# Attention ahead of two expert layers on one Trainium2 core: the turn back of a pair's outputs stands right ahead of the next pair's first products

## The chip, the core and the metric

The kernel runs on one core of a Trainium2 chip. It has five engines with a queue of instructions each: TensorE (PE in the profile; its weight loads are listed as PEld), VectorE (DVE), ScalarE (ACT), GpSimd (POOL) and SyncE (SP), which here issues most transfers. Engines wait for each other by semaphores alone. The metric is the time of one execution on the device in microseconds (us), the median of several runs; less is better.

## The reference, cut to what matters

Attention with normalized queries and keys, four batches of twelve heads, 448 tokens, 64 numbers a head; its output goes through a layer of eight experts of which each token takes one, and then through a dense layer of two matrices. The change lies in the attention alone.

```python
q_n, k_n = (rmsnorm(q, g_q), rmsnorm(k, g_k))
scores = scale * np.matmul(q_n, k_n.transpose(0, 1, 3, 2))
scores = scores - np.max(scores, axis=-1, keepdims=True)
attn = np.exp(scores)
attn = attn / (np.sum(attn, axis=-1, keepdims=True) + 1e-09)
return np.matmul(attn, v).astype(np.float32)
...
x = _moe_ref(x=x, **moe_kwargs)
return _moe2_ref(x=x, **moe2_kwargs)
```

## The kernel before

Attention goes by 24 pairs of heads. The 2 x 448 tokens of a pair are seven blocks of 128 (the fourth holds the last 64 tokens of both heads). The loop `for n in range(N)` runs over 168 steps, seven for each pair. In step n it writes out, in this order: the transpositions of one block of probabilities of the pair before (`turn_p`, line 306, into the tile "pt"), the scores of one block (`scores`, line 286, into "s"), the exponential of the block of the step before (`expo`, line 297, ScalarE), the copy of the transposed block out of PSUM (`take_p`, lines 326 and 328, ScalarE or VectorE), the maximum of the new block (`row_max`, line 291, VectorE), and then what the table `sched` holds for this step. There is no scheduler behind it: each engine works through its instructions in the order in which they are written, and a function that is put at a step adds its instructions to the queues of all engines that it uses, at that place.

The table is filled by `put(z + off, f, p)`, with z = 7p the first step of pair p's scores. What matters here, in steps 0 to 6 of the pair whose scores are being computed:

- `turn_k` (line 234) transposes the seven blocks of k on TensorE, four of them in step 2 and three in step 4, two pairs ahead or less, and ScalarE takes the high part (line 236); `k_low` (line 241) on VectorE takes the low part from the same PSUM tile "tk", in step 3 for the first four and in step 5 for the other three. After `k_low` nothing reads that tile.
- `turn_q` (line 217) transposes blocks of q in steps 5 and 3 into a PSUM tile "tq", which ScalarE copies out (lines 219, 222, 223).
- `mix` multiplies v with the transposed probabilities into the tile "av": blocks 0, 4, 1 and 5 in step 4 (line 338, weights of 128x64), the rest in step 6 (lines 338 and 342). `mixed` (line 347) copies the sum to the tile "osb" in step 6.
- `back`, the turn back, brings a pair's outputs, which have tokens along the columns, back to tokens along the rows, and multiplies them with the router's weights in the same passes: six full-size passes (three matmuls, line 363) and four quarter-size ones (two matmuls, line 365, weights of 64x64) into the PSUM tile "xo". `finish` calls `finish_pair`, in which VectorE scales the result in three operations (lines 1605, 1607, 1608). After a batch's last pair SyncE stores the batch (lines 1611, 1614), and the router's work on it is added in small pieces to later steps.

A float32 matmul stands in the profile as two passes with a weight load each, so the three matmuls of line 363 are six there. The tiles tk, tq and xo, and small ones of the router, belong to one PSUM group with the name "tq" and two buffers: a new tile takes a buffer that a former one has had, and its first matmul waits until the former one's last reader is done. The first pairs are placed by the table `place`, since the stage starts there; the last steps, with the turn back of pairs 22 and 23, are written out by hand behind the loop.

Of the kernel before, what the change touches and what calls it, by code (L numbers as in the profile page):

```python
# [32 lines left out]
def attention(tc, ctx, q, k, v, const, ps, late, finish_pair, tick, early):  # L33
# [352 lines left out]
    def put(n, f, p, *a):  # L386
        m = place.get(p, {}).get(f.__name__, n)
        sched.setdefault(m if type(m) is int else m[a[0]], []).append((f, (p,) + a))
# [13 lines left out]
    for p in range(NP):  # L402
        z = 7 * p
        put(z + 11, mix, p, (0, 1))
        put(z + 13, mix, p, (2, 3))
        for off, f in ((-16, scale_k), (-15, scale_q), (-13, q_high), (-12, q_low), (13, invert), (13, mixed), (15, back), (15, finish)):
            put(z + off, f, p)
        put(z - 7, load, p, "v")
        if 1 < p < 4:
            put(z - 14, copy_k, p)  # L410
        for off, f, i in ((-9, turn_q, 0), (-5, turn_k, 0), (-4, turn_q, 1), (-4, k_low, 0), (-3, turn_k, 1), (-2, k_low, 1)):
            put(z + off, f, p, i)
# [1122 lines left out]
def tile_kernel(ctx: ExitStack, tc: tile.TileContext, q, k, v, g_q, g_k, moe_modality_id, moe_w_gate, moe_modality_bias,  # L1535
                moe_w1, moe_w2, moe2_w_in, moe2_w_out, out):
    nc = tc.nc
    with tc.manual_schedule():
# [8 lines left out]
        with ExitStack() as c0:  # L1547
# [87 lines left out]

            moe.ident = moe.m.ident = ident
            attention(tc, c0, q, k, v, dict(ident=ident, identr=identr, comb=comb, gg=gg), ps, late, finish_pair, tick, lambda i: moe.early(i))
        moe.run(steps)

# [30 lines left out]
```

## Time and profile before

| | us |
|---|---|
| median of 3 runs | 1143.63 |
| lowest and highest | 1143.36, 1143.73 |
| the profiled execution | 1144.76 |
| its span, first to last instruction | 1142.8 |
| TensorE busy in the span | 1124.5 (98%) |
| VectorE, ScalarE, GpSimd busy | 822.6, 677.7, 368.4 |

Attention takes about the first 335 us of the span; the steady run of its steps is the stretch from 40 to 334 us. The sum of the busy times of an engine says little by itself; in the timeline a row is one or several equal instructions in a line, with the start of the first, the time until the end of the last, and in brackets how long the engine had been idle before and what ended that. Matmuls overlap, so the cost of one is the distance from its start to the next one's start.

### The profile page before, as it was taken

What the parts mean: (1) busy time and instruction counts of PE and PEld (TensorE: products, weight loads), DVE (VectorE), ACT (ScalarE), POOL (GpSimd) and SP (SyncE); (2) the same over time, 40 slices, a digit from 0 to 9 for tenths busy, and PEclk for the clock granted to TensorE, in tenths of its full rate; (3) what the DMA queues carried; (4) which work ended last, traced back from release to release, by engine and by line L of the source; (5) the groups of instructions that cost most, each with busy time, mean ns of one, the idle gap of its engine ahead of it and who ended that gap; (6) DMA issues with size and microseconds to landing.
All of it is one profiled execution on the core that took longest, in us unless ns stands there. A gap on an engine that the chain in (4) does not pass through costs nothing. (4 is left out here: it accounts for less than half of the span.)

```text
span 1142.8 us, 20023 instructions
## 1 busy us (share of the span) xinstructions
PE 1124.5 (98%) x7101; PEld 952.3 (83%) x7101; DVE 822.6 (72%) x1537; ACT 677.7 (59%) x1374; POOL 368.4 (32%) x559
## 2 busy tenths in 40 slices
PE   7999999999999999999999999999999999999997
PEld 6767777776768998999999988888888888888996
DVE  7887877867767667898989978884544455444674
ACT  6887777777654566666565555554543454433664
POOL 4575656644213204345644434430200010000100
PEclk9999999999999999999999999999999999999999
DMA  4343334213336789998999723330200011000100
GB/s 108 80 105 107 80 79 118 66 49 96 96 104 209 238 261 315 287 321 286 299 286 298 248 79 110 99 123 1 111 1 1 1 42 42 1 1 1 56 1 28
DMA packets 144708, 138.12 MB, mean 121 GB/s; under 512 B 39254, under 2 KB 125270, under 8 KB 144092
## 3 DMA queue, kind: packets, MB, share of 16 engines
q1 hardware_dynamic: 140444, 120.24, 34.7%
q0 software_dynamic: 4000, 16.53, 4.1%
q8 instruction: 57, 0.93, 0.4%
q14 instruction: 47, 0.39, 0.1%
q10 hardware_dynamic: 160, 0.03, 0.0%
HBM read 117.23 MB, written 18.10 MB: 118 GB/s over the span
## 5 line engine op out<-in xcount | busy, mean ns | idle before, releaser
L965 DVE TENSOR_TENSOR l<-ld,h 128x768 fp32r<-128x768 f32 x157 | 149.4, 968 | 18.7 <-ACT h L960 16.0
L1005 PE MATMUL a<-h,gh 128*128 128x512 f32 x476 | 159.4, 340 | 0.0
L1005 PE MATMUL a<-h,gl 128*128 128x512 f32 x476 | 157.7, 337 | 0.0
L1005 PE MATMUL a<-l,gh 128*128 128x512 f32 x476 | 157.7, 337 | 0.0
L937 POOL TENSOR_SCALAR cva<-cva 128x384 f32<-128x384 f32 x64 | 108.2, 1692 | 142.8 <-ACT cva L936 142.6
L960 ACT ACTIVATE h<-ld 128x768 fp32r<-128x768 f32 x159 | 130.6, 840 | 16.6 <-PE hs L984 6.5
L1479 POOL DMA_INDIRECT out_dram<-ld,oidx x11 | 12.8, 1159 | 334.4 <-DVE ld L1477 179.9
L297 ACT ACTIVATE P<-s,nb 128x448 f32<-128x448 f32 x144 | 91.7, 637 | 30.4 <-DVE nb L291 26.0
L291 DVE TENSOR_REDUCE nb<-s 128x1 f32<-128x448 f32 x168 | 102.9, 615 | 8.9 <-PE s L286 8.2
L1423 ACT ACTIVATE u<-hp,half 128x512 f32<-128x512 f32 (+1 forms) x64 | 40.4, 632 | 106.2 <-PE hp L973 106.2
L1430 DVE SCALAR_TENSOR_TENSOR w<-u 128x512 f32<-128x512 f32 (+1 forms) x64 | 40.2, 629 | 84.9 <-ACT u L1423 84.9
L1005 PEld LDWEIGHTS a<-h,gl 128*128 128x128 f32 x476 | 89.0, 189 | 10.7
L1005 PEld LDWEIGHTS a<-h,gh 128*128 128x128 f32 x476 | 89.0, 189 | 10.6
L1005 PEld LDWEIGHTS a<-l,gh 128*128 128x128 f32 x476 | 88.9, 189 | 9.6
L328 DVE COPY pT<-pt 128x448 f32<-128x448 f32 x96 | 59.8, 623 | 51.1 <-PE pt L306 51.1
L973 PE MATMUL hp<-yh,h 128*128 128x512 f32 (+1 forms) x384 | 88.5, 366 | 0.4 <-PEq L1372 0.4
L973 PE MATMUL hp<-yl,h 128*128 128x512 f32 (+1 forms) x384 | 87.2, 362 | 0.0
L973 PE MATMUL hp<-yh,l 128*128 128x512 f32 (+1 forms) x384 | 87.2, 362 | 0.0
L1438 DVE TENSOR_TENSOR gl<-u,gh 128x512 fp32r<-128x512 f32 (+1 forms) x64 | 40.0, 625 | 61.4 <-ACT gh L1437 61.4
L1181 ACT ACTIVATE rh<-hp 128x256 fp32r<-128x256 f32 x64 | 24.6, 384 | 100.3 <-PE hp L973 100.3
L306 PE MATMUL pt<-ident,P 128*128 128x128 f32 x504 | 83.4, 274 | 0.4 <-ACT P L297 0.2
L1437 ACT ACTIVATE gh<-u 128x512 fp32r<-128x512 f32 (+1 forms) x64 | 36.9, 577 | 77.5 <-PE a L1005 75.0
(345 smaller groups left out, 2821.0 us busy)
## 6 DMA issues: line engine op xcount, KB each, us to landing
ld<-in_moe_w_dram SPq DMA_DIRECT2D x160, 384.0 KB
raw<-in_moe_w_in_dram SPq DMA_DIRECT2D x32, 384.0 KB
ld<-in_moe_w_out_dram SPq DMA_DIRECT2D x26, 384.0 KB
rawk<-in_k_dram SPq DMA_DIRECT2D x24, 192.0 KB
rawq<-in_q_dram SPq DMA_DIRECT2D x24, 192.0 KB
rawv<-in_v_dram SPq DMA_DIRECT2D x24, 192.0 KB
xt_d<-x SPq DMA_DIRECT2D x4, 1152.0 KB
kn<-kn SPq DMA_DIRECT2D x20, 224.0 KB
```

The lines of the kernel that those rows point to most:

```text
L291: nc.vector.tensor_reduce(out=R["nb"][:, u:u + 1], in_=R["s", u], op=ALU.max, axis=AX.X, negate=True)
L297: nc.scalar.activation(out=o, in_=R.pop(("s", u)), func=ACTF.Exp, bias=R["nb"][:, u:u + 1], accum_out=R["sum"][:, w:w + 1])
L306: nc.tensor.transpose(out=out, in_=src, identity=ident)
L328: nc.vector.tensor_copy(out=R["PT", m], in_=t)
L937: nc.gpsimd.tensor_scalar(out=R["a"], in0=R["a"], scalar1=2.0 ** -15, scalar2=122879.9921875, op0=ALU.max, op1=ALU.min)
L960: nc.scalar.activation(out=h, in_=src, func=ACTF.Copy)
L965: (engine or self.nc.vector).tensor_tensor(out=l, in0=src, in1=h.bitcast(F32), op=ALU.subtract)
L973: nc.tensor.matmul(out=t[:, 0:n], lhsT=w[:, k], rhs=x[:, k, 0:n], start=i == 0 and k == 0, stop=i == 2 and k == 5)
L1005: nc.tensor.matmul(out=a[2][:, 256 * j:256 * j + 256] if c else a[j], lhsT=p[:, t * 128:t * 128 + 128], rhs=q[:, 512:768] if c else q[:, 0 ...
L1423: nc.scalar.activation(out=u, in_=t[:, s], func=ACTF.Relu, scale=0.5, bias=half)
L1430: nc.vector.scalar_tensor_tensor(out=w, in0=u, scalar=1.0, in1=u, op0=ALU.min, op1=ALU.mult)
L1438: nc.vector.tensor_tensor(out=gl[:, 0:n], in0=u, in1=gh[:, 0:n].bitcast(F32), op=ALU.subtract)
```

## The change

In the table, the offset of `back` and `finish` goes from 15 to 18. So the turn back of pair p leaves step 1 of pair p+2 and stands in step 4 of that pair. The `mix` of blocks 0, 4, 1 and 5 of pair p+1 is put at the same step (7(p+1) + 11 = 7p + 18) and comes behind it, since the table is filled pair by pair. For p up to 21 the step lies in the loop; pairs 22 and 23 are in the part written by hand, which is the same.

```diff
-        for off, f in ((-16, scale_k), (-15, scale_q), (-13, q_high), (-12, q_low), (13, invert), (13, mixed), (15, back), (15, finish)):
+        for off, f in ((-16, scale_k), (-15, scale_q), (-13, q_high), (-12, q_low), (13, invert), (13, mixed), (18, back), (18, finish)):
             put(z + off, f, p)
```

TensorE, step 1 of pair 11, where pair 9's turn back stood (s: scores, kh, kl and Q: the transposed k and q, xo: the turn back's tile, osb: the pair's outputs; a semaphore in brackets is one that the instruction waits for, by the engine that raises it). Before:

```order
L286 MATMUL s_2559<-kl_2401,Q_2280 128x448
L363 MATMUL xo_2569<-comb_89,osb_2521 128x144 [waits DVE_49]
L363 MATMUL xo_2569<-comb_89,osb_2521 128x144 x2
L365 MATMUL xo_2569<-comb_89,osb_2521 64x72 x2
L306 MATMUL pt_2580<-ident_70,pm1_274 128x128 [waits DVE_49]
L306 MATMUL pt_2580<-ident_70,P_2326 128x128 x3
```

The same place with the change:

```order
L286 MATMUL s_2559<-kh_2391,Q_2280 128x448
L286 MATMUL s_2559<-kl_2392,Q_2280 128x448
L306 MATMUL pt_2571<-ident_70,pm1_274 128x128 [waits DVE_49]
L306 MATMUL pt_2571<-ident_70,P_2326 128x128 x3
L286 MATMUL s_2576<-kh_2391,Q_2280 128x448
```

The two rows of the turn back are gone; the transpositions follow the scores.

TensorE, step 4 of the same pair, where the first products of pair 10 stand (av, from pT, the transposed probabilities, and rawv). Before:

```order
L286 MATMUL s_2626<-kh_2400,Q_2280 128x448 [waits Activation_49]
L286 MATMUL s_2626<-kl_2401,Q_2280 128x448
L338 MATMUL av_2633<-pT_2475,rawv_2145 64x448 [waits DMAHW2_49]
L338 MATMUL av_2633<-pT_2589,rawv_2145 64x448
L338 MATMUL av_2633<-pT_2506,rawv_2145 64x448
L338 MATMUL av_2633<-pT_2612,rawv_2145 64x448 [waits Activation_49]
```

With the change:

```order
L286 MATMUL s_2617<-kh_2391,Q_2280 128x448 [waits Activation_49]
L286 MATMUL s_2617<-kl_2392,Q_2280 128x448
L363 MATMUL xo_2624<-comb_89,osb_2521 128x144 [waits DVE_49,PE_49]
L363 MATMUL xo_2624<-comb_89,osb_2521 128x144 x2
L365 MATMUL xo_2624<-comb_89,osb_2521 64x72 x2
L338 MATMUL av_2633<-pT_2475,rawv_2145 64x448 [waits DMAHW2_49]
L338 MATMUL av_2633<-pT_2580,rawv_2145 64x448
L338 MATMUL av_2633<-pT_2506,rawv_2145 64x448
L338 MATMUL av_2633<-pT_2603,rawv_2145 64x448 [waits Activation_49]
```

The turn back stands between the scores and the products. Its first matmul waits for VectorE and for TensorE's own earlier writes; by the program's counts the VectorE instruction is the `k_low` of kl_2584 below.

VectorE, steps 1 to 4 of the same pair (nb: row_max, kl: k_low, x, lg and xt: the scaled outputs). Before:

```order
L291 TENSOR_REDUCE nb_2532<-s_2559 128x1 [waits PE_49]
L1605 TENSOR_TENSOR x_1954<-xo_2569,r_2519 128x3x128 [waits DVE_49,PE_49]
L1607 TENSOR_TENSOR lg_1956<-xo_2569,r_2519 128x7x8
L1608 TENSOR_SCALAR xt_1955<-xo_2569,r_2519 128x64
L328 COPY pT_2589<-pt_2580 128x448 [waits PE_49]
L291 TENSOR_REDUCE nb_2532<-s_2585 128x1 [waits PE_49]
L291 TENSOR_REDUCE nb_2532<-s_2606 128x1 [waits PE_49]
L241 SCALAR_TENSOR_TENSOR kl_2593<-tk_2594,gg_92,kh_2592 128x512 [waits Activation_49]
L328 COPY pT_2630<-pt_2621 128x448 [waits PE_49]
L291 TENSOR_REDUCE nb_2532<-s_2626 128x1 [waits PE_49]
```

With the change:

```order
L291 TENSOR_REDUCE nb_2532<-s_2559 128x1 [waits PE_49]
L328 COPY pT_2580<-pt_2571 128x448 [waits PE_49]
L291 TENSOR_REDUCE nb_2532<-s_2576 128x1 [waits PE_49]
L291 TENSOR_REDUCE nb_2532<-s_2597 128x1 [waits PE_49]
L241 SCALAR_TENSOR_TENSOR kl_2584<-tk_2585,gg_92,kh_2583 128x512 [waits Activation_49]
L328 COPY pT_2621<-pt_2612 128x448 [waits PE_49]
L291 TENSOR_REDUCE nb_2532<-s_2617 128x1 [waits PE_49]
L1605 TENSOR_TENSOR x_2037<-xo_2624,r_2519 128x3x128 [waits DVE_49,PE_49]
L1607 TENSOR_TENSOR lg_2039<-xo_2624,r_2519 128x7x8
L1608 TENSOR_SCALAR xt_2038<-xo_2624,r_2519 128x64
```

The three scaling operations move behind the row_max of step 4, past two copies, three row_max and the k_low.

On SyncE the stores of lines 1611 and 1614 stay where they were in its queue; ScalarE's and GpSimd's instructions keep their order.

## Rows read from the trace of the kernel before

**Rows 1.** Table by stretches: length; busy PE, PEld, DVE, ACT, POOL; clock; DMA share; GB/s.

```profile
12.00:18.00 6.00, 4.54 (x19) 3.73 (x20) 4.29 (x11) 4.17 (x12) 3.10 (x13) 0.72 0.45 86
40.00:334.00 294.00, 293.10 (x2008) 210.71 (x2006) 223.78 (x566) 220.51 (x588) 154.33 (x334) 1.00 0.31 85
```

**Rows 2.** TensorE's waits, 40 to 334 us: total us, times, longest.

```profile
PE pt L306 <- ACT pT L326: 0.2, 1, 0.2
```

**Rows 3.** Timeline, TensorE, pair 9's turn back: start, us, operation.

```profile
157.73 0.37 PE L286 MATMUL s<-kl,Q 128*128 128x448 f32 x1
157.94 0.90 PE L363 MATMUL xo<-comb,osb 128*128 128x144 f32 x6
158.76 0.34 PE L365 MATMUL xo<-comb,osb 64*64 64x72 f32 x4
159.04 0.33 PE L306 MATMUL pt<-ident,pm 128*128 128x128 f32 x1
159.20 0.49 PE L306 MATMUL pt<-ident,P 128*128 128x128 f32 x3
```

**Rows 4.** Timeline, TensorE, a step without a turn back.

```profile
182.16 0.37 PE L286 MATMUL s<-kl,Q 128*128 128x448 f32 x1
182.37 0.38 PE L306 MATMUL pt<-ident,pm 128*128 128x128 f32 x2
182.58 0.54 PE L306 MATMUL pt<-ident,P 128*128 128x128 f32 x3
```

**Rows 5.** Timeline, TensorE, steps 3 and 4 after pair 9's turn back.

```profile
161.43 0.37 PE L286 MATMUL s<-kl,qm 128*128 128x448 f32 x1
...
162.52 0.36 PE L286 MATMUL s<-kl,Q 128*128 128x448 f32 x1
162.81 1.72 PE L338 MATMUL av<-pT,rawv 128*64 128x448 f32 x8
```

**Rows 6.** Timeline, VectorE, the same steps, idle time in brackets.

```profile
159.16 0.56 DVE L1605 TENSOR_TENSOR x<-xo,r 128x384 f32<-128x384 f32 x1 [0.39 <-PE xo L365]
...
159.75 0.28 DVE L1608 TENSOR_SCALAR xt<-xo,r 128x64 f32<-128x64 f32 x1
...
161.84 0.62 DVE L291 TENSOR_REDUCE nb<-s 128x1 f32<-128x448 f32 x1 [0.75 <-PE s L286]
162.38 0.74 DVE L241 SCALAR_TENSOR_TENSOR kl<-tk,gg,kh 128x512 fp32r<-128x512 f32 x1
```

**Rows 7.** Timeline, first products and tile's reader, pairs 2, 6, 7, 8, 20.

```profile
71.21 1.84 PE L338 MATMUL av<-pT,rawv 128*64 128x448 f32 x8
...
72.40 0.24 ACT L223 ACTIVATE qm<-tq 128x64 fp32r<-128x64 f32 x1
...
122.98 0.97 PE L338 MATMUL av<-pT,rawv 128*64 128x448 f32 x4
...
122.77 0.74 DVE L241 SCALAR_TENSOR_TENSOR kl<-tk,gg,kh 128x512 fp32r<-128x512 f32 x1
...
136.12 1.35 PE L338 MATMUL av<-pT,rawv 128*64 128x448 f32 x6
...
136.38 0.74 DVE L241 SCALAR_TENSOR_TENSOR kl<-tk,gg,kh 128x512 fp32r<-128x512 f32 x1
...
149.27 0.97 PE L338 MATMUL av<-pT,rawv 128*64 128x448 f32 x4
...
149.20 0.73 DVE L241 SCALAR_TENSOR_TENSOR kl<-tk,gg,kh 128x512 fp32r<-128x512 f32 x1
...
305.64 0.60 PE L338 MATMUL av<-pT,rawv 128*64 128x448 f32 x2
...
305.35 0.49 ACT L219 ACTIVATE Q<-tq 128x384 fp32r<-128x384 f32 x1
```

**Rows 8.** Timeline, VectorE and TensorE's weight loads, a wait for k_low.

```profile
72.72 0.74 DVE L241 SCALAR_TENSOR_TENSOR kl<-tk,gg,kh 128x512 fp32r<-128x512 f32 x1
...
73.52 0.31 PEld L234 LDWEIGHTS tk<-ident,kn 128*128 128x128 f32 x3 [0.23 <-DVE kl L241]
```

## The prediction

> **What bounds the kernel now.** First the table by stretches: from 40 to 334 us, the attention stage in its steady run, TensorE is busy for 293.10 of 294.00 us at a granted clock of 1.00, which is its 2.4 GHz level; VectorE has 223.78 and ScalarE 220.51 [rows 1]. Then what TensorE waited for in that stretch: one entry of 0.2 us [rows 2]. So the stage is one queue of TensorE instructions without holes, in which the other engines' results are always there in time. Two things follow. What the change saves on TensorE itself is saved from the span, and any wait that it puts into that queue is added to the span in full, since no later hole takes it up. The timeline of TensorE around one turn back is the third view: the distances from start to start, not the busy times, are what an instruction costs there. The fourth is VectorE's timeline in the same steps.
>
> A pair of heads takes seven steps. I call them steps 0 to 6 of the pair whose scores are computed. Before, the turn back of pair p stands at the end of step 1 of pair p+2; now it stands in step 4 of pair p+2, right ahead of the first products of pair p+1. The move is made for pairs 0 to 21. Pairs 22 and 23 stand in the hand-written tail in both kernels.
>
> **The change part by part.**
>
> *What leaves step 1.* From the last scores matmul to the first turn-back matmul 0.21 us, six full-size ones 0.82, the four quarter-size ones 0.28 until the next transposition starts, and that first transposition takes 0.16 to the next one [rows 3]. Where scores are followed by transpositions directly, it is 0.21 and then 0.21 for two, so 0.105 for one [rows 4]. So 0.21 + 0.82 + 0.28 + 0.16 becomes 0.21 + 0.105: **1.155 us less**.
>
> *What enters step 4.* Scores to the first product takes 0.29 us now [rows 5]. It becomes 0.21 + 0.82 to the quarter-size matmuls and then their step to the products. No row shows quarter-size weights (64x64) followed by the products' half-size ones (128x64). The nearest row is quarter-size to full-size, 0.28 [rows 3]; a change of size between scores and products costs 0.29 where none costs 0.21 [rows 4, 5], and what follows the first instruction after one starts 0.055 later (0.16 for 0.105). I take 0.28: **1.02 us more**. Had this passage no price of its own, it would be about 0.135 less per pair, 3.0 us in all. By the Trainium skill (TensorEngine Tiling (Array Packing), Key Properties) a change of the tiling mode drains TensorE, and moving on within one mode does not; 64x64 and 128x64 are two modes there, so by that rule too the passage has its price.
>
> Balance of TensorE's own work: 1.02 - 1.155 = -0.135 us a pair, for 22 pairs **-3.0 us**. Were this all, the change would be a small gain.
>
> *The wait that it brings.* The turn back writes a tile of the PSUM group "tq", which has two buffers. In step 1 its buffer was last read by an operation of an earlier pair's step 5, long done. In step 4 it takes the buffer that the four transposed k tiles of pair p+3 used in step 2, and the last reader of those is VectorE's k_low (line 241), which stands in step 3. For pair 0 and pairs 5 to 19, 16 in all, the first turn-back matmul now waits for just this instruction; for pairs 2 and 20 it waits for ScalarE's copies of a q tile (lines 219 to 223) of step 3; pairs 1, 3, 4 and 21 get no such wait. TensorE works its queue in order, so products, k transpositions and the next scores all stand behind the waiting matmul, and with them ScalarE and VectorE, which live on the scores. The question is whether these readers are done when TensorE gets there, and the trace of before has the time of both. TensorE would be ready 0.21 us after the last scores matmul of step 4, that is 0.08 ahead of the present first product.
>
> For pair 9: ready at 162.52 + 0.21 = 162.73 [rows 5]; k_low ends at 162.38 + 0.74 = 163.12 [rows 6]. **It is 0.39 us late.** And it can't come earlier: row_max ahead of it started after 0.75 us in which VectorE waited for the scores [rows 6], which began at 161.43 [rows 5]. From there the chain is scores 0.41, row_max 0.54 to the start of k_low, k_low 0.74: 1.69 us to its end, while TensorE needs 1.30 to be ready. Taking the turn back out of step 1 moves both sides by the same amount.
>
> The other pairs, ready being 0.08 ahead of the row of the products and the end being that of the reader [rows 7]: pair 6 123.51 - 122.90 = 0.61; pair 7 137.12 - 136.04 = 1.08; pair 8 149.93 - 149.19 = 0.74. These three come again with the router's work on VectorE after every sixth pair: 6, 12 and 18 as pair 6; 7, 13 and 19 as pair 7; 8 and 14 as pair 8. The other seven of the 15 are as pair 9, and pair 0 is taken so too. Pair 2: 72.64 - 71.13 = 1.51; pair 20: 305.84 - 305.56 = 0.28. Sum: 8 x 0.39 + 3 x 0.61 + 3 x 1.08 + 2 x 0.74 + 1.51 + 0.28 = **11.5 us**.
>
> A wait of this very kind stands once in the trace of before: k_low ends at 72.72 + 0.74 = 73.46, and TensorE's next weight load starts at 73.52 [rows 8], 0.06 later. The second instruction after an empty array starts 0.055 later than usual [rows 3, 4]. 18 waits x 0.115 = **2.1 us**.
>
> *What else moves.* VectorE's three scaling operations go along, out of steps 1 and 2, where they occupy it from 159.16 to 160.03, 0.87 us, into step 4 behind row_max. The next q transpositions (step 5) wait for the last of the three. It ends 2.09 us after the first turn-back matmul [rows 3, 6]; TensorE has 0.82 + 0.28 of turn back, 1.72 of products [rows 5] and then the k transpositions to do before step 5 begins, at least 2.8. So that is covered by 0.7 us; without it, it would be a second wait in the same pairs. The two stores at the end of a batch go three steps later on SyncE's queue, three times in all, with nothing of the next steps behind them; the router's first matmul stays in its step, because it waits for a fixed one. The order on ScalarE and GpSimd is unchanged.
>
> **Sum:** 11.5 + 2.1 - 3.0 = +10.6 us. The profiled execution took 1144.76 us, so 1155.4 for one like it; the median of the runs is 1.13 lower, 1143.63, which gives **1154.2 us**.
>
> *Bounds.* VectorE freed of 0.87 us in step 1 could bring the eight late kinds down to the ordinary 0.39, but not below, as its wait for the scores shows: -(3 x 0.22 + 3 x 0.69 + 2 x 0.35) = -3.4. A passage without a price: -3.0. On the other side TensorE reaches the place 1.155 earlier against the rest of the pair while VectorE gains only 0.87: 0.29 more for each of the eight and for pairs 2 and 20, +2.9, and I add 0.4 for the one short wait of [rows 2], should it come twice more in the tightened steps 2 and 3. The lower end takes three quarters of the two gains, the upper all of the loss: **1149.4 to 1157.5 us**.
>
> **The rivals.**
>
> *k_low is there in time (the other side).* VectorE no longer has the three scaling operations ahead of it, so k_low would end at least 0.39 us earlier against TensorE, no wait remains, and only the balance counts: -3.0 us, 1140.6. It decides at a k_low that ends no later than the last scores matmul plus 0.21 us. For it speaks that in pairs 6, 7 and 8 VectorE ran without a gap. Against it: in pair 9 it sat idle for 0.75 us ahead of row_max and was late all the same [rows 6]. Chance 0.05.
>
> *Only the crowded pairs wait.* If the seven ordinary pairs and pair 0 lost their wait by some shift of the steps, their 8 x (0.39 + 0.115) = 4.0 us would go; if the late kinds also fell by 0.39 and the prices of waking there stayed, 3.1 more, and +3.5 would remain, and with the passage without a price +0.5: about 1144 to 1147. The same rows speak against it. Chance 0.04, half of it within 0.2%.
>
> *The clock falls.* Early in the kernel TensorE does wait: between 12 and 18 us it is busy for 4.54 of 6.00 us, and the granted clock is 0.72 on average over these 6 us, so part of them ran at the lower level, 1.2 GHz [rows 1]. Such a spell loses 6.00 x 0.28 = 1.7 us. If the new waits brought one in each of 22 pairs, that is +37 us on top, about 1191. Against it: the new waits are a half to one us in some 13, 4% of the time instead of the 24% of that stretch. The Trainium skill describes this outcome (TensorE: Matmul & The Clock Gate, A second HAM failure mode: psum-queue depth-cycling): a queue that cycles through PSUM banks idles TensorE so often in short spells that the clock swings; no row of before shows it in the steady stage. Chance 0.03.
>
> **How the numbers follow.** The forecast, waits about as long as read, has the remaining 0.88. A measurement of this kernel tells about 0.2%, 2.3 us, from no change. Faster by more than that is the first rival alone, 0.05. Within it is half of the second, 0.02. Slower is the forecast, the other half and the clock: 0.93. The range holds the forecast but for its tails and leaves the rivals out: 12% for them and some 8% for the tails.
>
> **What would show it.** In the profile after, TensorE's list of waits should have a new entry, xo of line 363 released by kl of line 241, about 16 times with a mean near 0.5 us, and one or two by ScalarE's lines 219 to 223; the stretch from the first to the last turn back should be some 10 us longer and everything behind it only shifted; the products should follow the quarter-size matmuls at 0.28 us (0.17 or less would show a passage without a price); the granted clock should stay 1.00 there. The prediction is wrong if that entry is missing, if k_low ends before TensorE asks for its buffer, or if the span grows elsewhere.

## The result and the profile after

The changed kernel takes 1158.53 us (median of 4 runs, 1157.99 to 1160.04), the kernel before in the same comparison 1143.49 us (4 runs, 1143.11 to 1143.73). The ratio is 1.0132 (95% interval 1.0119 to 1.0144), so it is slower by 15.0 us. The forecast was 1154.2, its range ended at 1157.5: the sign and the foreseen wait were right, the size was 4.3 us short. The profiled execution of after took 1158.31 us with a span of 1156.2.

TensorE's waits in the attention stage, 40 to 350 us, where before had the one entry of [rows 2] (waited in total, times, longest):

```profile
PE xo L363 <- DVE kl L241: 8.0, 16, 0.9
PE xo L363 <- ACT qm L223: 1.6, 1, 1.6
PE tk L234 <- DVE kn L192: 1.0, 1, 1.0
PE pt L306 <- ACT pT L326: 0.9, 4, 0.3
PE pt L306 <- DVE pT L328: 0.6, 1, 0.6
```

And the table by stretches, columns as in [rows 1]:

```profile
40.00:347.00 307.00, 295.00 (x2003) 209.64 (x2004) 221.50 (x566) 215.31 (x587) 154.10 (x334) 1.00 0.29 81
```

The first two entries of the waits are the foreseen ones. The other three are new or larger than before, and the forecast had none of them in its sum. TensorE is now idle for 12 of 307 us where it had 0.9 of 294, and the granted clock is still 1.00. The last turn back starts at 347.49 us instead of 333.11, 14.4 us later; the loss is made before it. (The 0.6 us between that and the 15.0 of the medians lie within the interval, 13.6 to 16.5 us. The spans of the two profiled executions differ by 13.4; single runs of after differ by 2.0 among themselves.)

Pair 9's turn back at its new place, the place of [rows 5] and [rows 6]; TensorE first, then VectorE (start, us, operation, idle time before in brackets):

```profile
166.86 0.36 PE L286 MATMUL s<-kl,Q 128*128 128x448 f32 x1
167.61 0.98 PE L363 MATMUL xo<-comb,osb 128*128 128x144 f32 x6 [0.40 <-DVE kl L241]
168.52 0.34 PE L365 MATMUL xo<-comb,osb 64*64 64x72 f32 x4
168.79 1.72 PE L338 MATMUL av<-pT,rawv 128*64 128x448 f32 x8
...
166.19 0.62 DVE L291 TENSOR_REDUCE nb<-s 128x1 f32<-128x448 f32 x1 [1.04 <-PE s L286]
166.73 0.74 DVE L241 SCALAR_TENSOR_TENSOR kl<-tk,gg,kh 128x512 fp32r<-128x512 f32 x1
```

TensorE is ready at 166.86 + 0.21 = 167.07, k_low ends at 166.73 + 0.74 = 167.47: 0.40 late, as read beforehand (0.39). The matmul starts 0.14 after that end, and the six of its kind take 168.52 - 167.61 = 0.91 instead of 0.82. The step from the quarter-size matmuls to the products is 0.27.

To see where the 14.4 us lie, I took the start of the last scores matmul of each step, in each profiled execution, and compared its distance to the next one with that of before. The turn back of pair p stands in the steps of pair p+2, called scored pair p+2 below; a pair without that word is numbered by its turn back. Only three distances change: step 1 to 2 (the old place), 2 to 4, and 4 to 5 (the new place); in e4, where work is filled in, also step 0 to 1. Sums over scored pairs 2 to 23, us against before:

| kernel | ratio of the runs | step 1 to 2 | 2 to 4 | 4 to 5 | whole stage |
|---|---|---|---|---|---|
| forecast for after | 1.0092 | -25.4 | 0 | +36.0 | +10.6 |
| after | 1.0132 | -23.5 | +2.2 | +35.8 | +14.2 |
| e1_sgroup | 1.0018 | -23.5 | +2.2 | +23.9 | +2.5 |
| e2_behind | 1.0062 | -23.5 | +2.3 | +28.8 | +7.3 |
| e3_klow | 1.0054 | -23.4 | +2.2 | +26.9 | +5.4 |
| e4_fill (and +26.4 of filling) | 1.0327 | -25.5 | -0.3 | +37.1 | +37.5 |
| e5_part | 0.9996 | -18.4 | +1.7 | +16.3 | -0.5 |
| e6_part_v | 1.0044 | -18.4 | +3.6 | +20.2 | +5.3 |
| e7_before_v | 1.0020 | 0.0 | +1.9 | +0.1 | +1.9 |
| e8_after_v | 1.0167 | -23.5 | +4.1 | +38.1 | +18.7 |
| e9_chosen | 1.0016 | -15.0 | +2.4 | +14.9 | +2.1 |
| e10_moved_copy | 0.9988 | -15.0 | +0.5 | +13.2 | -1.5 |

(The whole stage is from the first to the last scores matmul; what is missing from a line's sum is the start of the stage, within 0.4 us.) So the new place costs what was forecast, 35.8 for 36.0. What was missing is at the old place: 1.9 us that step 1 did not give back, and 2.2 us behind it.

Three views of after show the missing 4.1 us. **Pair 0, step 1**: two rows of TensorE, one of VectorE and one of GpSimd, then TensorE of before at the same point:

```profile
39.21 0.37 PE L286 MATMUL s<-kl,Q 128*128 128x448 f32 x1
40.60 0.65 PE L234 MATMUL tk<-ident,kn 128*128 128x128 f32 x4 [1.02 <-DVE kn L192]
...
39.40 1.15 DVE L192 COPY kn<-kn 128x448 f32<-128x448 f32 x1
...
39.32 0.94 POOL L198 TENSOR_TENSOR qn<-rawq,y 128x448 f32<-128x448 f32 x1
```

```profile
39.75 0.53 PE L363 MATMUL xo<-comb,osb 128*128 128x144 f32 x3
40.21 0.34 PE L365 MATMUL xo<-comb,osb 64*64 64x72 f32 x4
40.68 0.63 PE L234 MATMUL tk<-ident,kn 128*128 128x128 f32 x4
```

VectorE's copy ends at 40.55 in after, and it ended at the same time before:

```profile
39.39 1.15 DVE L192 COPY kn<-kn 128x448 f32<-128x448 f32 x1
```

Before, TensorE did the turn back until about then; now it stands idle for the copy, and step 1 of this pair gives back 0.08 us, not 1.155.

**Pair 21, step 1**: the same with VectorE's copy of a block of pT; the step gives back 0.34. Rows of after, then of before:

```profile
326.43 0.37 PE L286 MATMUL s<-kl,Q 128*128 128x448 f32 x1
...
326.73 0.61 DVE L328 COPY pT<-pt 128x448 f32<-128x448 f32 x1
...
327.40 0.33 PE L306 MATMUL pt<-ident,pm 128*128 128x128 f32 x1 [0.60 <-DVE pT L328]
```

```profile
313.04 0.37 PE L286 MATMUL s<-kl,Q 128*128 128x448 f32 x1
...
313.34 0.62 DVE L328 COPY pT<-pt 128x448 f32<-128x448 f32 x1
...
314.35 0.33 PE L306 MATMUL pt<-ident,pm 128*128 128x128 f32 x1
```

The copy ends 0.92 us after the last scores of step 1 before and 0.91 after. TensorE came to the next transposition 1.31 us after those scores before, a margin of 0.39; with 1.155 us less it is 0.77 late, and 0.81 of the step's gain is missing.

**Pair 8, step 2**, the strongest of the many small ones: TensorE and ScalarE of after, then of before:

```profile
148.63 0.36 PE L286 MATMUL s<-kl,Q 128*128 128x448 f32 x1
...
149.67 0.60 PE L234 MATMUL tk<-ident,kn 128*128 128x128 f32 x4
150.49 0.33 PE L306 MATMUL pt<-ident,pm 128*128 128x128 f32 x1 [0.22 <-ACT pT L326]
...
149.23 0.64 ACT L297 ACTIVATE P<-s,nb 128x448 f32<-128x448 f32 x1 [0.89 <-DVE nb L291]
...
149.85 0.59 ACT L326 ACTIVATE pT<-pt 128x512 f32<-128x512 f32 x1
```

```profile
144.09 0.36 PE L286 MATMUL s<-kl,Q 128*128 128x448 f32 x1
...
146.73 0.27 PE L306 MATMUL pt<-ident,pm 128*128 128x128 f32 x1
...
145.32 0.59 ACT L326 ACTIVATE pT<-pt 128x512 f32<-128x512 f32 x1
```

ScalarE's copy frees the PSUM tile that the transposition of step 3 writes. It ends 145.91 - 144.09 = 1.82 us after the last scores of step 1 before, and 150.44 - 148.63 = 1.81 after: it hangs on scores that were queued ahead of the old turn back and does not come earlier. TensorE asked for the tile after 146.73 - 144.09 = 2.64 us, a margin of 0.82. With 1.155 us of work taken out in between, the margin is -0.33.

### The profile page after: what moved, and what is told of

The parts are those of the page before. It is cut to its first block, busy times and chain, and to the rows that moved or that the text cites. A ratio compares the mean times of both kernels' runs of the same rounds, so it can differ in the third digit from the quotient of the medians.

```text
span 1156.2 us, 19990 instructions
## 1 busy us (share of the span) xinstructions
PE 1127.8 (98%) x7101; PEld 952.2 (82%) x7101; DVE 821.0 (71%) x1537; ACT 673.1 (58%) x1374; POOL 366.4 (32%) x559
```

## The experiments

**Is it the tile's group? (e1)** The turn back at its new place writes group "s" (three buffers) instead of "tq".

```diff
-        t = ps.tile([128, 7, 72], F32, name="xo", tag="tq")
+        t = ps.tile([128, 7, 72], F32, name="xo", tag="s", bufs=3)
```

> The changed kernel, but the turn back's tile is taken from the PSUM group of the scores ("s", three buffers) instead of "tq" (two). It then waits for ScalarE's exponential of the scores of step 2, which in pair 9 of the changed kernel ends at 166.81 us where TensorE is ready at 167.07. Theory A (the price is the wait for k_low, the last reader of the tq buffer): the 18 waits in step 4 cost 35.8 - 22 x 1.01 = 13.6 us in the changed kernel's trace; they go but for some in the crowded pairs, so 1145 to 1147.5 us, 11 to 13.5 less than the changed kernel, and step 4 is 1.01 longer than before in nearly all pairs. Theory B (taking the turn back out of step 1 tightens steps 1 to 3, and what is late there is late for any buffer): another wait takes its place, 1154 or more.

Measured: 1146.88 us, ratio 1.0018 (1.0009 to 1.0028). The wait for k_low is gone from the list, and the new place costs 1.01 to 1.02 us in pairs 5 to 21 (1.16 to 1.65 in pairs 0 to 4, with two waits for ScalarE's exponentials of line 297, the readers of group "s", 0.9 us). TensorE in pair 9:

```profile
163.38 0.36 PE L286 MATMUL s<-kl,Q 128*128 128x448 f32 x1
163.59 0.90 PE L363 MATMUL xo<-comb,osb 128*128 128x144 f32 x6
164.41 0.34 PE L365 MATMUL xo<-comb,osb 64*64 64x72 f32 x4
164.69 0.60 PE L338 MATMUL av<-pT,rawv 128*64 128x448 f32 x2
```

That is 0.21 + 0.82 + 0.28, the terms of the forecast to the hundredth. The buffer was the cause of the wait: 35.8 - 23.9 = 11.9 us are gone. But the rest is not the gain of 3.0 us that TensorE's own balance promised: the losses in steps 1 and 2 stay as they were, so they belong to the old place.

**The turn back behind the products (e2)**, in the same step and the same group: by then k_low should be done.

```diff
+        if p:
+            put(z + 11, back, p - 1)
+            put(z + 11, finish, p - 1)
...
-        for off, f in ((-16, scale_k), (-15, scale_q), (-13, q_high), (-12, q_low), (13, invert), (13, mixed), (18, back), (18, finish)):
+        for off, f in ((-16, scale_k), (-15, scale_q), (-13, q_high), (-12, q_low), (13, invert), (13, mixed)):
```

> The turn back stays in step 4 with its tile in tq, but behind the first products of the next pair instead of ahead of them. The products take 1.66 us, the lateness of k_low is 0.4 to 1.1 us, so it is hidden. Theory A: no wait in step 4; the balance of TensorE's own work against the kernel before is 0.82 + 0.28 + 0.055 in, 1.155 out, so 0 a pair; what steps 1 and 2 lose (4.1 us in the changed kernel's trace) stays: 1147.6, 11 us less than the changed kernel. Theory B: as the changed kernel within 2 us, 1156 to 1159.

Measured: 1151.63 us, ratio 1.0062 (1.0045 to 1.0079). No wait of xo is left in the list, but the step grows by 1.20 us in 19 pairs and by 1.84 to 2.08 in pairs 1, 2 and 4, where the next q tile is copied later by ScalarE (a new entry, tk for the line 219 copy, 1.7 us in 3 times). The expectation priced TensorE's own work in this order at 1.155 us, so the 19 pairs came out 0.05 above it and the three others 0.7 to 0.9. The wait for k_low was avoided: 28.8 - 22 x 1.155 = 3.4 us above the bare work are left, most of them waits at the next hand-over of the buffer in three pairs, against 13.6 in after. The total lies between theory A's 1147.6 and theory B's 1156.

**k_low one step earlier (e3)**, so that it is done when xo asks:

```diff
-        for off, f, i in ((-9, turn_q, 0), (-5, turn_k, 0), (-4, turn_q, 1), (-4, k_low, 0), (-3, turn_k, 1), (-2, k_low, 1)):
+        for off, f, i in ((-9, turn_q, 0), (-5, turn_k, 0), (-4, turn_q, 1), (-5, k_low, 0), (-3, turn_k, 1), (-2, k_low, 1)):
```

> The changed kernel with k_low of the first four k tiles put at the end of step 2 instead of step 3, so that VectorE does it ahead of step 3's row_max. Theory A with the chain scores, row_max, k_low as what sets its end: k_low then ends with ScalarE's high part plus 0.8 us, 167.07 in pair 9 where TensorE is ready at 167.07; of the 0.4 us in the ordinary pairs nearly all goes, in the crowded ones some: 6 to 9 us less than the changed kernel, 1149.5 to 1152.5. If row_max ahead of it is not what makes it late: no change, 1157 to 1160. A loss would mean that the delayed row_max (0.8 us) is waited for in its turn.

Measured: 1150.54 us, ratio 1.0054 (1.0037 to 1.0071). That is in theory A's range. The growth of step 4 falls from 1.64 to 2.12 us to between 1.12 and 1.20 in pairs 5 to 19. In pair 1 it rises from 1.01 to 1.78, and in pair 2 it stays at 2.38: there the three k blocks of step 4 wait for ScalarE's copy of q (tk for line 219, 1.2 us in 2 times, a new entry). Pair 9, TensorE and VectorE:

```profile
164.74 0.36 PE L286 MATMUL s<-kl,Q 128*128 128x448 f32 x1
165.01 1.00 PE L363 MATMUL xo<-comb,osb 128*128 128x144 f32 x6
...
164.21 0.75 DVE L241 SCALAR_TENSOR_TENSOR kl<-tk,gg,kh 128x512 fp32r<-128x512 f32 x1 [1.18 <-ACT kh L236]
```

k_low ends at 164.96 where TensorE is ready at 164.95: just on time, and yet the matmul starts 0.06 late and the six take 0.93 instead of 0.82. So a wait that only just happens still costs 1.19 - 1.02 = 0.17 us a pair, of which the list of waits shows nothing.

**Filling in the old place (e4)**: 11 transpositions without use ahead of step 1's scores, about as long as the turn back was.

```diff
-        for _ in range(fill.get(7 * p + u, 0)):
+        for _ in range(fill.get(7 * p + u, 0) + (11 if u == 1 and 2 <= p else 0)):
```

> The changed kernel with eleven transpositions that nobody reads ahead of the scores of step 1, in the 22 pairs from which the turn back was taken: about as much TensorE work as left that step, 22 x 11 x 0.105 = 25.4 us. Theory A' (the turn back in step 1 covered other waits, of the transposed blocks for ScalarE's copy and of pair 3's k for its copy on VectorE; 4.1 us of the loss in steps 1 and 2 are these): the fill takes 4.1 us of waits away, so 21.3 us more than the changed kernel, 1179.8, and steps 2 as long as before. If those losses have another cause: 25.4 more, 1183.9.

Measured: 1181.95 us, ratio 1.0327 (1.0310 to 1.0345). The total lies between the two expectations and alone decides nothing. The filling took 1.20 us a pair, 26.4 in all, where 25.4 was priced; and the list of waits now has the turn back waiting for ScalarE's copies of q (9.3 us in 10 times and 1.6 in 2) instead of k_low, which makes 1.3 us more in step 4. The single steps do decide: step 1 gives back 1.15 to 1.17 us in every pair from 1 on (pair 21: 1.17, it was 0.34) and 1.27 in pair 0, and from step 2 to 4 no pair loses more than 0.1. Against after that is 26.4 + 1.3 - 2.0 - 2.5 = 23.2 us, and the two stages differ by 37.5 - 14.2 = 23.3. With some work back at the old place, all three losses are gone: what the turn back did there was cover.

**Only where it pays (e5)**: e1 for pairs 5 to 20, the old place for the others.

```diff
-        t = ps.tile([128, 7, 72], F32, name="xo", tag="tq")
+        t = ps.tile([128, 7, 72], F32, name="xo", tag="s", bufs=3) if 5 <= p <= 20 else ps.tile([128, 7, 72], F32, name="xo", tag="tq")
...
-            put(z + off, f, p)
+            put(z + (15 if off == 18 and not 5 <= p <= 20 else off), f, p)
```

> The turn backs of pairs 5 to 20 stand at the new place and write a tile of the PSUM group "s" (three buffers); those of pairs 0 to 4 and 21 stay at the end of step 1 in group "tq". Theory cover: the turn back at its old place also covered waits of step 1 (pairs 0 and 21) and of step 2 (pairs 4 to 21); keeping the old place at both ends saves the 1.9 us of step 1, and over pairs 5 to 20 the gain of 1.155 in step 1 is eaten by 1.02 in step 4 and by about 0.1 a pair of lost cover in step 2: sum -0.5, ratio 0.9996 against before, 1143.0 against 1143.5. Rival: the losses of steps 1 and 2 belong to the new place wherever it is used (they follow from the tile's buffers), and some +1.5 to +2.5 us remain as with the variant in group "s" for all pairs.

Measured: 1143.95 us against 1144.20, ratio 0.9996 (0.9987 to 1.0006), as the cover theory said. Of the 2.1 us that 16 pairs should win, 1.7 are eaten in step 2.

**Who is late in step 2? (e6, e7, e8)** If it is ScalarE's copy of block 3, giving it to VectorE, which lost 0.87 us of work there [rows 6], should free it. The same edit on e5 (e6), on before (e7) and on after (e8):

```diff
-        if m in (1, 3, 5):
+        if m in (1, 5) or m == 3 and not 6 <= p <= 21:
```

> As the variant for pairs 5 to 20 with group "s"; besides, the step-1 block of transposed probabilities (block 3) of scored pairs 6 to 21 is copied out of PSUM by VectorE instead of ScalarE. Theory cover: the waits of step 2 are for ScalarE's copy of that block, which starts late behind ScalarE's exponentials; VectorE has room in step 1, since it lost the three scaling operations there, so the losses of step 2 fall away, -1.6 us: ratio 0.9982, 1141.4. Rival: VectorE's 0.5 us more per pair delays row_max, and with it ScalarE and the next transpositions, by as much or more in the crowded pairs (6 to 8 and their repeats): 0 to +3 us against the variant without it, 1143 to 1146.

> The kernel before with only the block-3 copy of scored pairs 6 to 21 moved from ScalarE to VectorE. Theory cover: before, TensorE waited for that copy once for 0.2 us in the whole stage, so there is nothing to win: -0.2 to 0; and VectorE, which still has the scaling operations there, may come late in the crowded pairs: up to +2. Rival: ScalarE's copy limits before too (its cover is thin), and the kernel gains 1 us or more by the move alone.

> The changed kernel with only the block-3 copy of scored pairs 6 to 21 moved from ScalarE to VectorE. Theory cover: the part of the step-2 losses that lies in these pairs, 1.7 us, falls away, and the waits for k_low stay as they are: 1156.8 against 1158.5. Rival: VectorE's 0.5 us more in step 1 makes k_low later in the eight crowded pairs, where VectorE has no gap: +4 us on the k_low waits, 1160 to 1161.

Measured: e6 1148.94 us, ratio 1.0044 (1.0030 to 1.0058); e7 1146.44, 1.0020 (1.0010 to 1.0029); e8 1162.83, 1.0167 (1.0152 to 1.0181). The cause is confirmed; in e6 and e8 the total goes to the rival, and e7 loses 1.9 us in the stage, the upper end of what the cover theory allowed. In e6 and e8 the loss from step 2 to 3 is gone in all pairs concerned (between -0.02 and +0.01, it was up to +0.43). But in the crowded pairs the next two steps lose more than that: pair 8 in e8 loses 1.10 from step 3 to 4 and its step 4 grows from 1.64 to 2.00. Rows of e8 there, TensorE, VectorE and GpSimd:

```profile
153.62 0.33 PE L306 MATMUL pt<-ident,pm 128*128 128x128 f32 x1 [1.02 <-DVE pT L328]
...
155.44 0.97 PE L363 MATMUL xo<-comb,osb 128*128 128x144 f32 x6 [0.76 <-DVE kl L241]
...
151.57 1.00 DVE L133 TENSOR_SCALAR yi<-m 128x28 int32<-128x28 int32 x1
...
152.95 0.62 DVE L328 COPY pT<-pt 128x448 f32<-128x448 f32 x1
...
151.38 1.15 POOL L208 TENSOR_TENSOR qs<-qn,qs 128x448 fp32r<-128x448 f32 x1 [0.44 <-ACT qs L203]
```

VectorE comes to the small operation of line 133 0.48 us later than in after, counted from the last scores of step 1, and GpSimd to its line 208 0.48 earlier, since ScalarE, without the copy, makes the input of line 208 earlier. In after line 133 stood 0.77 us ahead of line 208; now it finds it running and ends right after it (152.57 and 152.53). The copy behind it comes late, and TensorE waits for it for a microsecond. The totals of e6 and e8 are even above the rival's numbers: what looked like half a microsecond moved between two engines cost 0.3 to 1.1 us from step 3 to 4 in five of the pairs, and 0.4 to 0.6 more in their step 4, since VectorE had no slack there. In before (e7) the same pairs, 8 and 14, lose 0.71 each in the same way: line 133 takes 0.99 us there, begun 0.19 behind line 208.

**A version put together from single pairs (e9, e10)**: the new place with group "s" for pairs 5 to 7, 9 to 13 and 15 to 19; VectorE's copy only in scored pairs 7, 11 to 13 and 17 to 19 (e9), then in 6, 10 to 12 and 16 to 18 (e10). The diff is against e5; e10 has the other list of pairs in the first line.

```diff
-        if m in (1, 3, 5):
+        if m in (1, 5) or m == 3 and p not in (7, 11, 12, 13, 17, 18, 19):
...
-        t = ps.tile([128, 7, 72], F32, name="xo", tag="s", bufs=3) if 5 <= p <= 20 else ps.tile([128, 7, 72], F32, name="xo", tag="tq")
+        t = ps.tile([128, 7, 72], F32, name="xo", tag="s", bufs=3) if 5 <= p <= 19 and p not in (8, 14) else ps.tile([128, 7, 72], F32, name="xo", tag="tq")
...
-            put(z + (15 if off == 18 and not 5 <= p <= 20 else off), f, p)
+            put(z + (15 if off == 18 and not (5 <= p <= 19 and p not in (8, 14)) else off), f, p)
```

> The turn backs of pairs 5 to 7, 9 to 13 and 15 to 19 stand at the new place and write group "s"; the other nine stay at the old place in group "tq". The block-3 copy is moved to VectorE in scored pairs 7, 11 to 13 and 17 to 19 alone, where it cost nothing in the run for pairs 5 to 20. If gains and losses are those of each pair, as read from the tables of the two runs for pairs 5 to 20 (-0.14 to -0.18 us in nine pairs, -0.02 to -0.16 in the rest), the sum is -1.6 us: ratio 0.9986, 1141.9. Rival: the losses hang on the row of pairs (a pair at the old place between two at the new one shifts the buffers of groups s and tq and so the waits), and some +1 to +3 us come in around pairs 8 and 14: 1144 to 1146.

Measured: 1146.58 us, ratio 1.0016 (1.0007 to 1.0025): not the forecast. The size is the rival's, but the place is not quite: the steps of scored pairs 8, 14 and 20 lost 1.0, 1.0 and 0.8 us. I had misread which pair a copy belongs to; the copy of scored pair 7 falls into the steps of scored pair 8.

> As the chosen version, with VectorE's copy one pair earlier: scored pairs 6, 10 to 12 and 16 to 18. In the chosen version the copies of pairs 7, 13 and 19 cost 0.6 us in step 3 of the next pair and 0.6 in its step 4, since block 3 of a pair's probabilities is transposed in step 1 of the pair after it; the copy that helps the row of scored pair n is that of pair n-1. If that is all, the rows of scored pairs 8, 14 and 20 fall back to -0.16, those of 11 and 17 from +0.02 to -0.18, and the sum is -1.6 us: ratio 0.9986, 1142.9 against 1144.5. Rival: the rise of 0.6 and 0.6 comes from the old place of pairs 8 and 14 beside the new one; then the rows of scored pairs 8, 14 and 20 stay at +0.8 to +1.0 and the ratio at 1.0010 or more.

Measured: 1143.26 us against 1144.63, ratio 0.9988 (0.9979 to 0.9997). Those three pairs are back at -0.16 us. All of TensorE's waits from 40 to 334 us are one line

```profile
PE pt L306 <- ACT pT L326: 0.4, 2, 0.3
```

The whole stage wins 1.5 us. This is the only version whose interval lies below 1, by about a thousandth and with its end at 0.9997, and it needs a place, a buffer group and a copying engine chosen pair by pair from the runs before it.

## Why the prediction was right in direction and short in size

*TensorE's own work.* Right. Step 1 gives back 1.14 to 1.18 us in 20 of 22 pairs (1.155 said); the move costs 1.01 in the four pairs without a wait (1.02 said). The passage that no row of before showed, quarter-size to half-size weights, is 0.27 (0.28 taken). The Trainium skill's rule on the drain at a change of tiling mode (TensorEngine Tiling (Array Packing), Key Properties) agrees with that number.

*The wait for k_low.* Right in place and count: 16 times, plus one long wait for ScalarE's qm; the short one of pair 20 shows in its step alone, which grew by 1.37. Taken from the steps, waits and waking cost 35.8 - 22 x 1.01 = 13.6 us, and 11.5 + 2.1 = 13.6 was said. That the sums agree is luck, since two errors cancel. Waking costs 0.23 a time, not 0.115: in pair 9, 0.14 from the end of k_low to the matmul and 0.09 more for the six (the 0.055 of the prediction was read behind a change of size, not behind a wait). And the crowded pairs and pair 2 were less late than read: step 4 in pairs 8 and 14 grew by 1.64 where 1.875 was said, in 7, 13 and 19 by 2.09 to 2.12 for 2.215, in pair 2 by 2.43 for 2.645. For the crowded pairs this lies within the bounds given; for pair 2 no such bound was given. The list of waits shows 9.6 us of these 13.6; the rest is in distances between starts.

*The step that failed* is one clause of the part on the wait: "Taking the turn back out of step 1 moves both sides by the same amount", with the 0.4 us in the upper bound for the tightened steps 2 and 3. It holds for readers whose inputs are made behind the old place, as pair 9's k_low. It does not hold for results that hang on work queued ahead of the old place: there TensorE comes 1.155 us earlier and the result does not. For those the turn back was cover, the sum had nothing for its loss, and three kinds had less margin: the copy of kn in pair 0, a copy of pT in pair 21 (1.9 us together, 1.155 x 22 = 25.4 said, 23.5 found), and ScalarE's copy of block 3 in most pairs (2.2 us). Together 4.1 us, against a miss of 14.4 - 10.6 = 3.8 in the stage. The margins stood in the trace of before, 0.82 us in pair 8; I looked at the single wait that existed there [rows 2] and not at the waits that 1.155 us less would make. The filling (e4) shows that it is cover, e6 and e8 show whose it is in step 2.

*The balance as a gain.* The rival "k_low is there in time" priced the kernel without the wait at 1140.6. e1 is that case, and it came out 0.18% slower than before: 4.1 us of lost cover and 1.7 us of other waits at the new place are more than the gain of 22 x (1.155 - 1.01) = 3.2. Even without the wait for k_low, moving all 22 pairs wins nothing.

*The rivals.* k_low was not there in time, and the ordinary pairs did wait. The clock did not fall: 1.00 from 40 to 347 us, with waits up to 1.6 us in it. The Trainium skill's case of a clock that swings with short idle spells (TensorE: Matmul & The Clock Gate, A second HAM failure mode: psum-queue depth-cycling) does not show in the attention stage of any trace here: the granted clock is 1.00 from 40 us to the end of the stage in all twelve. The other moved steps cost nothing, as said: VectorE's scaling operations and the stores appear in none of TensorE's waits listed above.

## What to carry to other kernels

An instruction in a queue without holes is also cover for everything that is being made ready behind it: before taking it out, list for each of the next waits how long its result had been there, and price those with less margin than is taken away, also where the trace shows no wait at all. A tile's PSUM group decides whom a moved writer waits for, and the list of waits shows only a part of a wait's price, so measure step against step. Moving a copy from an engine that is late to one that is free on average pays only in the pairs in which that engine is free then.

## What the hardware showed beyond that

Two VectorE operations between SBUF tiles took several times as long when a GpSimd operation was running as they started. Minimum, median and longest of line 192 and of line 133 in after (ns), and of line 133 in e8:

```profile
L192 DVE COPY kn<-kn x3: 418/427/1145, 19.4 to 39.4; 128x448 f32<-128x448 f32 x3
L133 DVE TENSOR_SCALAR yi<-m x14: 163/170/384, 7.1 to 286.7; 128x28 int32<-128x28 int32 x10, 128x14 int32<-128x14 int32 x4
```

```profile
L133 DVE TENSOR_SCALAR yi<-m x14: 156/175/1108, 7.1 to 289.9; 128x28 int32<-128x28 int32 x10, 128x14 int32<-128x14 int32 x4
```

The long one of line 192 is pair 0's, 0.08 us behind the start of GpSimd's line 198 (the rows above); that of line 133 in pair 8 of e8 began 0.19 behind GpSimd's line 208. The Trainium skill has a rule for it (SBUF — State Buffer, Who interferes with whom): copies and tensor_scalar can take a port pair that VectorE shares with GpSimd, and who comes second is blocked until the other ends. The end of line 133, 0.04 us behind that of line 208, agrees; that of line 192 comes 0.29 behind line 198's and fits less closely. So a shift of VectorE by half a microsecond can change an operation's length, and not only its place.
